# Text-side edits in a two-stream attention block: shift sums folded after block transposes, text V shifted at its eviction, and the text gate's matmuls in the output phase

## The chip, the cores and the metric

The kernel runs on one core of a Trainium2 chip. The metric is device time in microseconds (us), median of five runs. In the text PE is TensorE with its matmuls, PEld its weight loads, DVE is VectorE, ACT is ScalarE, POOL is GpSimd, and SP is the engine whose queue issues most DMAs.

## The reference

There are two streams of tokens: image (B = 2 batches of 256 tokens) and text (2 of 32), with D = 1152. Weights and inputs are bfloat16.

```python
mod_i = (_silu(c) @ wmod_img).reshape(B, 6, 1, D)
mod_t = (_silu(c) @ wmod_txt).reshape(B, 6, 1, D)
shi, sci, gai = mod_i[:, 0], mod_i[:, 1], mod_i[:, 2]
sht, sct, gat = mod_t[:, 0], mod_t[:, 1], mod_t[:, 2]
hi = _layernorm(x_img) * (1 + sci) + shi
ht = _layernorm(x_txt) * (1 + sct) + sht
qkvi, qkvt = hi @ wqkv_img, ht @ wqkv_txt
q, k, v = concat of text and image parts
p = _softmax(einsum('bqd,bkd->bqk', q, k) * D ** -0.5)
a = einsum('bqk,bkd->bqd', p, v)
out_i = x_img + gai * (ai @ wo_img)
out_t = x_txt + gat * (at @ wo_txt)
```

So each stream needs a shift, a scale and a gate, each the product of the two silu(c) rows with a 1152 x 1152 slice of its modulation weights.

## The kernel before, in words

All work is on one core. D is cut into KT = 9 blocks of 128. Weights of 1152 x 1152 (2.65 MB) come from DRAM into five slots (w0 to w4); SP issues their DMAs in the order of lines 100 to 122, and a DMA whose slot is still in use waits on SP, with all behind it. `pin` keeps instructions in program order on their engine, so PE's order is the order of the code. The accumulators in PSUM come from two pools, ps_mm (six buffers) and ps_tr (two).

The stages, in PE's order:

1. Image LayerNorm, transposes, image scale and V (lines 296 to 342, `v_open`, `v_last`). The image shift is left out of the V input, and added later: `shift_v_rows` (391) multiplies the shift by the V weights, keeps the rows in `svr` (bfloat16) and as columns in `cols["v"]`, which the evictions of the attention output add to all tokens (L623, L625).
2. Image Q and K, nine blocks each (`qk_img`, 372), with hooks between blocks for text work: statistics and norm (402 to 412), transposes (414), scale rows (`txt_rows_scale`), shift, modulation.
3. Text Q and K (`qk_txt`, 478), scores and softmax (lines 646 to 668), the image gate (`img_gate`) between them, text V (`v_txt`, 489), transposes of the probabilities (`p_transposes`, 594), the text gate (`txt_gate`, 526), attention (`attn_pair`, 628), and the output products (679 to 718).

**Modulation rows.** A 32-column stationary operand holds silu(c) in two columns; four column groups of the array work on four strips of the weights at a time (`mod_rows_of`, 334): 36 matmuls of 288 columns for one product. **The text shift** goes another way: DVE multiplies each of the nine weight blocks by a per-partition scalar and adds (L425, L427, 18 instructions of 128x1152 for the two batches), which leaves sums over 128 partitions to do. ACT and DVE split the float32 sums into a high and a low bfloat16 half (`vec_split`, 430), and PE adds over the partitions with a one-column `pick` operand, 16 matmuls of 288 columns (`vec_rows`, 438); DVE transposes the result into columns (L229, L462).

**Text V.** Because the eviction of the attention output adds the image's shift row to every token, the text's V must have it subtracted: `v_txt` does that with four matmuls of `sel` (entries -1) and `svr` into the same accumulators. `v_txt_out` copies four strips into `v_t`, and L674 repeats the rows at partition 64, so that `attn_pair` can use four row groups.

**The gates.** `mod_rows` (506): 36 matmuls, an ACT copy `g_sb`, two POOL DMAs into a DRAM scratch (L515), and then POOL DMAs that read it back broadcast over partitions: `gb` for the image (L524), `gbf` for the text (L533). `xf` is the text input for the residual (L529). `out_txt` uses gbf and xf at L707 and L708.

**The text softmax.** `scores_txt` sums even and odd blocks in two halves of the partitions; ACT copies one half (L654), DVE adds (L657), takes the maximum (L554), ACT the exponential (L561), DVE divides into `pb_txt`, tile `pbt` (L568, L570). `p_transposes(0)` and `(1)` both read it.

Of the kernel before, what the change touches and what calls it, by code (L numbers as in the profile page):

```python
# [9 lines left out]
ALU = mybir.AluOpType  # L10
# [4 lines left out]
def kernel(  # L15
# [21 lines left out]
    P = 128  # L37
# [55 lines left out]
    def load_rows(slot, src, c0):  # L93
        t = wtile(slot)
        sv = wview(src, c0)
        for r0 in range(0, KT, 3):
            nc.sync.dma_start(t[:, r0:r0 + 3, :], sv[:, r0:r0 + 3, :])
        return t
# [14 lines left out]
    w_sh_t = load_rows(0, wmod_txt, 0)  # L113
# [6 lines left out]
    w_ga_t = load_w(2, wmod_txt, 2 * D)  # L120
    w_o_i = load_rows(3, wo_img, 0)
    w_o_t = load_rows(1, wo_txt, 0)
# [22 lines left out]
    pick = const.tile([P, B, 32], bf)  # L145
    nc.gpsimd.memset(pick[:], 0.0)
    for b in range(B):
        nc.gpsimd.memset(pick[:, b, b:b + 1], 1.0)
# [13 lines left out]
    nc.gpsimd.tensor_copy(ident2[:, P - NT:P], ident[:, 0:NT])  # L162

# [63 lines left out]
    def mod_cols_of(gps, name):  # L227
        t = const.tile([P, KT, LW], f32, name=name, tag={"shtc": "scc", "sctc": "shc"}.get(name, name))
        pin(nc.vector.transpose(t[:].rearrange("p c l -> p (c l)"), gps[:].rearrange("p c l -> p (c l)")))  # L229
        return t  # L230
# [124 lines left out]
    pin(nc.scalar.dma_start(x_t[:], xt_flat[:, :]))  # L355
# [16 lines left out]
    def qk_img(wq, blk, hooks):  # L372
        for j in range(KT):
# [3 lines left out]
            for kt in range(KT):  # L377
# [5 lines left out]
    sel = const.tile([P, NGG, NTT], bf)  # L383
    nc.gpsimd.tensor_scalar(sel[:].rearrange("p g (b t) -> p g b t", b=B),
                            ident[:].rearrange("p (g r) -> p g r", g=NGG)[:, :, 0:B].unsqueeze(3)
                            .to_broadcast([P, NGG, B, NT]), -1.0, None, op0=ALU.mult)
    v_t = act.tile([P, D], bf)
# [3 lines left out]
    def shift_v_rows():  # L391
        p_sv = mod_rows_of(w_v_i, shT32)
        nc.scalar.copy(svr[:], p_sv[:])
        cols["v"] = mod_cols_of(p_sv, "svc")

# [6 lines left out]
    def txt_stats():  # L402
        junk = v_t[0:NTT, :]
        pin(nc.scalar.activation(junk, x_t[:], ACT.Copy, scale=1.0 / D, accum_out=sm_t[0:NTT, 0:1]))
        pin(nc.scalar.activation(junk, x_t[:], ACT.Square, scale=float(D) ** -0.5, accum_out=sm_t[0:NTT, 1:2]))

    def txt_norm():
        pin(nc.vector.scalar_tensor_tensor(sm_t[0:NTT, 2:3], sm_t[0:NTT, 0:1], sm_t[0:NTT, 0:1], sm_t[0:NTT, 1:2],
                                           op0=ALU.mult, op1=ALU.subtract))
        rstd = ln_rstd(sm_t[0:NTT, 2:3], NTT, sign=-1.0)  # L410
        for h, (c0, c1) in enumerate(((0, KH * P), (KH * P, D))):
            ln_norm(x_t[:, c0:c1], sm_t[0:NTT, 0:1], rstd, NTT, xn_t[NTT * h:NTT * (h + 1), 0:c1 - c0])
# [8 lines left out]
    def vec_part(eng, w, acc, r0, r1, bs):  # L421
        for kt in range(r0, r1):
            for b in bs:
                if kt == 0:
                    pin(eng.tensor_scalar(acc[:, b, :], w[:, kt, :], sTf[:, kt, b:b + 1], None, op0=ALU.mult))  # L425
                else:
                    pin(eng.scalar_tensor_tensor(acc[:, b, :], w[:, kt, :], sTf[:, kt, b:b + 1], acc[:, b, :],  # L427
                                                 op0=ALU.mult, op1=ALU.add))

    def vec_split(acc):  # L430
        hl = work.tile([P, 2, B, D], bf, tag="hl", bufs=1, name="hl")
        halves[acc.name] = hl
        for b in range(B):
            nc.scalar.copy(hl[:, 0, b, :], acc[:, b, :])
            pin(nc.vector.tensor_sub(hl[:, 1, b, :], acc[:, b, :], hl[:, 0, b, :]))
        return hl

    def vec_rows(hl, gps, strip):
        terms = [(b, t) for b in range(B) for t in range(2)]
        for b, t in terms:  # L440
            for g in range(NGG):
                mm(gps[LW * g:LW * g + LW], lhsT=pick[:, b, :], rhs=strip(hl[:, t, b, :], g),
                   start=((b, t) == terms[0]), stop=((b, t) == terms[-1]), tile_position=(0, LW * g))
        return gps

    halves = {}
    acc_sh = act.tile([P, B, D], f32, tag="Bt")

    def txt_shift_part(r0, r1):
        return lambda: vec_part(nc.vector, w_sh_t, acc_sh, r0, r1, range(B))  # L450

    def txt_shift_split():
        vec_split(acc_sh)

    def txt_rows_shift():
        gps = ps_tr.tile([P, KT, LW], f32, tag="tr")
        rows["sh"] = vec_rows(halves[acc_sh.name], gps,
                              lambda a, g: a.rearrange("p (c g l) -> p g c l", g=NGG, l=LW)[:, g])

    def txt_cols_shift():  # L460
        cols["sh"] = mod_cols_of(rows["sh"], "shtc")
        nc.vector.tensor_copy(mod_t[:, 0], cols["sh"][:, :, 0:B])  # L462
# [4 lines left out]
    def txt_modulate():  # L467
        cols["sc"] = mod_cols_of(rows["sc"], "sctc")
        nc.vector.tensor_scalar_add(mod_t[:, 1], cols["sc"][:, :, 0:B], 1.0)
        h = hT_t[:].rearrange("p kt (b t) -> p (kt b) t", b=B)  # L470
        nc.vector.tensor_mul(h, xT_t[:].rearrange("p kt (b t) -> p (kt b) t", b=B),
                             mod_t[:, 1].rearrange("p kt b -> p (kt b)").unsqueeze(2).to_broadcast([P, KT * B, NT]))
        nc.vector.tensor_add(h, h,
                             mod_t[:, 0].rearrange("p kt b -> p (kt b)").unsqueeze(2).to_broadcast([P, KT * B, NT]))
# [14 lines left out]
    def v_txt(r):  # L489
        ps = ps_mm.tile([P, KT, LW], f32, tag="mm")  # L490
        for kt in range(KT):
            for g in range(2):
                mm(ps[64 * g:64 * g + NTT], lhsT=hT_t[:, kt, :], rhs=group(w_v_t, kt, 2 * r + g),
                   start=(kt == 0), stop=False, tile_position=(0, 64 * g))
        for g in range(2):
            mm(ps[64 * g:64 * g + NTT], lhsT=sel[:, 2 * r + g, :], rhs=svr[:],
               start=False, stop=True, tile_position=(0, 64 * g))
        return ps

    def v_txt_out(r, ps):  # L500
        for g in range(2):
            dst = v_t[0:NTT, :].rearrange("p (c g l) -> p g c l", g=NGG, l=LW)[:, 2 * r + g]
            src = ps[64 * g:64 * g + NTT]
            pin(nc.vector.tensor_copy(dst, src))
# [16 lines left out]
    def img_gate():  # L521
        mod_rows(w_ga_i, 0)
        for b in range(B):
            nc.gpsimd.dma_start(gb[:, b, :], gsc[0, b, :].partition_broadcast(P))  # L524

    def txt_gate():
        mod_rows(w_ga_t, 1)
        for g in range(2):
            pin(nc.gpsimd.dma_start(xf[64 * g:64 * g + NTT, :, :],  # L529
                                    xt_flat.rearrange("t (r g j) -> g t r j", r=2, g=2)[g]))  # L530
            for b in range(B):
# [6 lines left out]
    qk_img(w_q_i, 0, {1: (txt_stats, txt_shift_part(0, 3),), 3: (txt_norm,), 4: (txt_shift_part(3, 6),),  # L538
                      7: (txt_shift_part(6, KT),)})
    qk_img(w_k_i, 1, {1: (txt_transposes, txt_shift_split,),  # L540
                      6: (txt_rows_scale, txt_rows_shift, txt_cols_shift, txt_modulate),
                      8: (lambda: qk_txt(0, w_q_t),)})
# [51 lines left out]
    def p_transposes(b):  # L594
        pT_ps = ps_tr.tile([P, 8 * P], bf, tag="tr")

        def one(kj, pb, qp, perm):
            o = kj * NTOK + qp
            tr(pT_ps[:, o:o + P], pb[:, kj * P:(kj + 1) * P], perm[:])

        for kj in range(3):
            if b:
                one(kj, pbs["t"], qpos[b][2], ident2)
            for qi in range(TPB):
                one(kj, pbs[(b, qi)], qpos[b][qi], ident)
            if not b:
                one(kj, pbs["t"], qpos[b][2], ident)
        pT_v = pT_ps[:, 0:3 * NTOK].rearrange("p (k n) -> p k n", k=3)
        pT = work.tile([P, 3, NTOK], bf, tag="pT")
        pin(nc.scalar.copy(pT[:], pT_v))  # L610
# [17 lines left out]
    def attn_pair(ids0, ids1):  # L628
# [3 lines left out]
        for n, key in enumerate([x for pair in zip(t0, t1) for x in pair]):  # L632
            first, (b, dt) = key in t1, key
            r0 = 64 * (n // 2 % 2) + NT * b
            mm((t1 if first else t0)[key][:], lhsT=v_t[r0:r0 + NT, dt * P:(dt + 1) * P],
# [15 lines left out]
    soft_exp(I[1])  # L651
    st = scores_txt()
    half = work.tile([NTT, NTOK], f32, tag="half", bufs=1)
    pin(nc.scalar.copy(half[:], st[NTT:P, :]))  # L654
    img_div(I[1])
    img_gate()
# [12 lines left out]
    vt = [v_txt(r) for r in range(2)]  # L669
    v_txt_out(0, vt[0])  # L670
    p_transposes(0)
    p_transposes(1)
    v_txt_out(1, vt[1])
    pin(nc.vector.tensor_copy(v_t[64:64 + NTT, :], v_t[0:NTT, :]))  # L674
    txt_gate()
    for d0 in range(0, KT, 3):
        attn_pair(*[[(b, dt) for dt in range(d0, d0 + 3)] for b in range(B)])

    def out_img(i, chunks, parts=None):
# [4 lines left out]
        for n in chunks:  # L684
            ps = ps_mm.tile([P, CH], f32, tag="mm")
# [29 lines left out]
    out_img(1, C3)  # L715
# [33 lines left out]
```

## Time and profile before

| what | us |
|---|---|
| median of five runs | 119.0 (118.69 to 119.22) |
| the profiled execution | 118.93 |
| its span | 117.1 |
| PE busy | 110.8 (95%), 1046 matmuls |
| PE weight loads | 64.0 (55%) |
| DVE busy | 74.6 (64%) |
| ACT busy | 44.4 (38%) |
| POOL busy | 11.1 (10%) |
| DMA moved | 40.86 MB, mean 349 GB/s |

The page cuts the span in 40 slices and gives the busy share of each engine in tenths; PEclk is the clock granted to TensorE. The chain that ended last is followed back from the last instruction, and its shares tell on which engine it ran. The timeline gives start, duration, engine, line and shapes of each group; the idle time of the engine before it stands in brackets with what ended it. Times in a timeline are us from the span's start. A list of DMAs gives the time from issue to landing.

### The profile page before, as it was taken

Reading aid. Unit: us, or ns where it says so; the run is one execution under the profiler, and the core shown is the slowest. Engines: PE = TensorE matmul, PEld = TensorE weight load, DVE = VectorE, ACT = ScalarE, POOL = GpSimd, SP = SyncE. Lnnn points to the kernel's source line nnn. Section 1 sums busy time; section 2 is a strip of 40 time slices with the busy share of each in tenths; the row PEclk is TensorE's granted clock in tenths of the full one; section 3 lists DMA queues with packets and bytes.
Section 4 is the critical chain, followed back from the end, with each engine's and each line's share of the span. In section 5 each row is a group of like instructions: output and inputs, shape, how many; then the busy total and the mean of one; then the engine's idle time right before and its main releaser. Section 6 shows DMA issues by size and latency. Waiting matters only on the chain.

```text
span 117.1 us, 2513 instructions
## 1 busy us (share of the span) xinstructions
PE 110.8 (95%) x1046; PEld 64.0 (55%) x1054; DVE 74.6 (64%) x158; ACT 44.4 (38%) x91; POOL 11.1 (10%) x34
## 2 busy tenths in 40 slices
PE   4998799999999999999999999999999999999990
PEld 1245544445584444444444648777885666666660
DVE  2478395053865997999999350018994756666671
ACT  4799520031654815325248224245556620000000
POOL 7320000000000000000000000001309017000000
PEclk9999999999999999999999999999999999999999
DMA  3999999999999999999999999999999999420223
GB/s 118 388 376 398 404 406 408 414 412 412 412 400 372 412 410 412 406 410 414 412 411 412 412 406 410 413 408 408 411 403 412 406 395 348 147 101 6 101 50 101
DMA packets 18613, 40.86 MB, mean 349 GB/s; under 512 B 1019, under 2 KB 1547, under 8 KB 18603
## 3 DMA queue, kind: packets, MB, share of 16 engines
q1 hardware_dynamic: 17728, 39.56, 86.8%
q0 software_dynamic: 480, 0.89, 2.1%
q10 hardware_dynamic: 395, 0.26, 0.7%
q8 instruction: 8, 0.13, 0.4%
q14 instruction: 2, 0.02, 0.0%
HBM read 39.38 MB, written 1.34 MB: 348 GB/s over the span
## 4 chain that ended last, share of the span: by engine, by line
PE 85%; DMA 9%; DVE 1%; SPq 1%; issue 1%; DVEq 0%
PE ps L61 53%; PE vps L61 15%; DMA t<-in_wmod_img_dram 9%; PE gps L61 6%; PE aps L61 5%; PE sps L61 4%; PE pT_ps L64 1%; PE sc_ps L61 1%; SPq L104 1%; PE tp L64 1%; DVE tmp L690 1%; DVE o L691 0%; SPq L108 0%; PE tpt L64 0%; DVE hS_i L268 0%
## 5 line engine op out<-in xcount | busy, mean ns | idle before, releaser
L61 PE MATMUL ps<-xT_i,t 128*128 128x512 bf16 x157 | 35.2, 379 | 0.4 <-issue 0.2
L61 PEld LDWEIGHTS <-t 128*128 128x128 bf16 x324 | 20.5, 98 | 19.1 <-issue 0.5
L427 DVE SCALAR_TENSOR_TENSOR acc_sh<-t,sTf,acc_sh 128x1152 f32<-128x1152 bf16 x16 | 21.4, 1412 | 0.0
L61 PE MATMUL ps<-t,aT 128*128 128x384 bf16 (+3 forms) x153 | 20.2, 308 | 0.0
L61 PE MATMUL vps<-t,hS_i 128*128 128x512 bf16 (+1 forms) x106 | 17.8, 325 | 0.2
L61 PEld LDWEIGHTS <-aT 128*128 128x128 bf16 (+1 forms) x153 | 13.0, 101 | 7.1 <-issue 0.5
L61 PEld LDWEIGHTS <-hS_i 128*128 128x128 bf16 x108 | 9.0, 98 | 8.7 <-DVE hS_i L268 0.4
L690 DVE TENSOR_TENSOR tmp<-ps,gb 128x384 bf16<-128x384 f32 (+2 forms) x13 | 6.8, 525 | 6.4 <-PE ps L61 6.3
L370 ACT CAST qkT<-ps 128x512 bf16<-128x512 f32 (+2 forms) x11 | 6.0, 552 | 10.4 <-PE ps L61 10.4
L515 POOL DMA_DIRECT2D mod_scratch<-g_sb x4 | 2.5, 634 | 75.0 <-ACT g_sb L513 74.9
L368 ACT ACTIVATE qkT<-ps 128x512 bf16<-128x512 f32 (+2 forms) x11 | 6.0, 557 | 8.6 <-PE ps L61 8.6
L61 PE MATMUL wps<-warm 128*128 128x512 bf16 x24 | 7.7, 478 | 1.7 <-DVE unit L132 1.5
L184 DVE CAST v_i<-vps 128x512 bf16<-128x512 f32 x5 | 3.5, 692 | 7.5 <-PE vps L61 7.5
L554 DVE TENSOR_REDUCE nmx<-sps 128x1 f32<-128x288 f32 x4 | 1.8, 457 | 9.9 <-PE sps L61 9.9
L61 PEld LDWEIGHTS <-sT 128*32 128x32 bf16 x180 | 4.7, 96 | 3.0 <-issue 2.3
L186 ACT CAST v_i<-vps 128x512 bf16<-128x512 f32 x4 | 2.3, 578 | 9.9 <-PE vps L61 9.9
L623 DVE TENSOR_SCALAR aT<-aps,svc 128x288 bf16<-128x288 f32 x9 | 4.3, 518 | 2.5 <-PE aps L61 2.5
L61 PE MATMUL sps<-qkT 128*128 128x288 bf16 (+1 forms) x54 | 5.5, 287 | 0.0
L61 PEld LDWEIGHTS <-warm 128*128 128x128 bf16 x25 | 2.6, 115 | 5.2 <-issue 2.4
L61 PE MATMUL gps<-t,sT 128*32 128x288 bf16 x144 | 5.2, 287 | 0.0
L61 PE MATMUL aps<-pT,v_i 128*128 128x288 bf16 x36 | 5.1, 287 | 0.0
L61 PE MATMUL ps<-hT_t,t 128*128 128x64 bf16 x162 | 5.0, 193 | 0.0
(114 smaller groups left out, 109.2 us busy)
## 6 DMA issues: line engine op xcount, KB each, us to landing
t<-in_wqkv_txt_dram SPq DMA_DIRECT2D x3, 2592.0 KB, 18.0
t<-in_wmod_img_dram SPq DMA_DIRECT2D x2, 2592.0 KB, 12.6
t<-in_wqkv_img_dram SPq DMA_DIRECT2D x2, 2592.0 KB, 20.2
t<-in_wmod_txt_dram SPq DMA_DIRECT2D x2, 2592.0 KB, 16.2
t<-in_wmod_txt_dram SPq DMA_DIRECT2D x3, 864.0 KB, 15.2
t<-in_wo_img_dram SPq DMA_DIRECT2D x3, 864.0 KB, 13.1
t<-in_wo_txt_dram SPq DMA_DIRECT2D x3, 864.0 KB, 12.7
t<-in_wqkv_img_dram SPq DMA_DIRECT2D x3, 576.0 KB, 8.7
```

The costliest lines, as they stand in the source:

```text
L61: return pin(nc.tensor.matmul(*a, **k))
L64: return pin(nc.tensor.transpose(*a, **k))
L104: nc.sync.dma_start(x_i[:, b * TPB:(b + 1) * TPB, :], x_img[b].rearrange("(p t) d -> p t d", t=TPB))
L184: nc.vector.tensor_copy(out_ap, in_ap)
L186: nc.scalar.copy(out_ap, in_ap)
L368: nc.scalar.mul(out_ap, in_ap, SCALE)
L370: nc.scalar.copy(out_ap, in_ap)
L427: pin(eng.scalar_tensor_tensor(acc[:, b, :], w[:, kt, :], sTf[:, kt, b:b + 1], acc[:, b, :], op0=ALU.mult, op1=ALU.add))
L515: nc.gpsimd.dma_start(gsc[si, b, :].rearrange("(g j) -> g j", g=NGG), g_sb[b:P:32, :])
L554: pin(nc.vector.reduce_max(nmx[0:qn, :], sps[0:qn, :], axis=AX.X, negate=True))
L623: nc.vector.tensor_scalar(dst, tiles[(b, dt)][:], bias, None, op0=ALU.add)
L690: nc.vector.tensor_mul(tmp[:, 0:n], ps[:, 0:n], gb[:, b, c0:c0 + n])
```

## The change

- **Shift sums.** The nine blocks of products stay on DVE (`shift_part`). Then DVE transposes the float32 sums in 32 x 32 blocks and reduces along the free axis (`shift_blocks`), which leaves 36 partial sums for each batch and partition. These 72 columns are split in two bfloat16 parts, and two matmuls of 72 columns with a constant `fold` add over the four groups of 32 partitions; a mask `band` and a reduce pick the right column (`shift_fold`). The 16 pick matmuls, the ACT and DVE splits and one transpose go.
- **Place of the text modulation.** The scale rows come ahead of K block 4 (before: 6), the scale product follows `shift_blocks` on DVE, and fold and shift come ahead of K block 8. Text K now follows image K directly; text Q comes after the first two image scores; the image gate comes ahead of the text scores.
- **Text V.** `svr` goes through a DRAM scratch (POOL DMAs, L401 and L405 of the changed kernel) to `svb`, one row broadcast to the text's partitions. `v_txt` has no sel matmuls, reads contiguous columns and splits them over two halves of the partitions; one DVE subtraction for each accumulator (and a 64 x 64 one) writes `v_t`. The attention takes the output blocks in another order, (0, 5, 1), (6, 2, 7), (3, 8, 4), for the new layout.
- **Probability transposes.** `p_transposes(0)` comes before `v_txt`, `p_transposes(1)` after it, the latter in two tiles with two ACT copies, its third key block first.
- **Text gate.** `txt_gate` is called between the first and second chunk of `out_img(1)`; `xf` is loaded with the image gate.
- **Loads.** The text shift weights come in four DMAs instead of three; x_t comes on SP's queue behind them (before: ACT's queue); wo_img comes ahead of the text gate's weights and in slot 4; wo_txt in two DMAs.
- **Text LayerNorm.** The two normalizing instructions go from DVE to ACT.

```diff
+    w_sh_t = load_rows(0, wmod_txt, 0, (0, 1, 3, 6))
+    nc.sync.dma_start(x_t[:], xt_flat[:, :])
...
-    w_ga_t = load_w(2, wmod_txt, 2 * D)
-    w_o_i = load_rows(3, wo_img, 0)
-    w_o_t = load_rows(1, wo_txt, 0)
+    w_o_i = load_rows(4, wo_img, 0)
+    w_ga_t = load_w(3, wmod_txt, 2 * D)
+    w_o_t = load_rows(1, wo_txt, 0, (0, 5))
...
+    fold = const.tile([P, NGG, LW], bf)
+    nc.gpsimd.tensor_add(fold[:, 0, :], ident[:, 0:LW], ident[:, LW:2 * LW])
...
+        for b in range(B):
+            nc.gpsimd.dma_start(svd[b].rearrange("(c g l) -> g c l", g=NGG, l=LW), svr[b:P:LW])
+        for g in range(2):
+            for b in range(B):
+                r0 = 64 * g + NT * b
+                nc.gpsimd.dma_start(svb[r0:r0 + NT, :], svd[b, g * HD:(g + 1) * HD].partition_broadcast(NT))
...
+    def shift_blocks():
         for b in range(B):
+            blk = work.tile([P, NB, LW], f32, tag="blk", bufs=1, name="blk")
+            pin(nc.vector.transpose(blk[:].rearrange("p c l -> p (c l)"), acc_sh[:, b, :]))
+            pin(nc.vector.reduce_sum(uf[:, b, :], blk[:], axis=AX.X))
+        pin(nc.vector.tensor_copy(ub[:, 0], uf[:]))
+        pin(nc.vector.tensor_sub(ub[:, 1], uf[:], ub[:, 0]))
+
+    def shift_fold():
+        ps = ps_tr.tile([P, B * KT, NGG], f32, tag="tr", name="shps")
+        for h in range(2):
+            mm(ps[:].rearrange("p k a -> p (k a)"), lhsT=fold[:].rearrange("p g l -> p (g l)"),
+               rhs=ub[:, h].rearrange("p b c -> p (b c)"), start=(h == 0), stop=(h == 1))
+        pin(nc.vector.tensor_mul(uf[:].rearrange("p b (k a) -> p (b k) a", a=NGG), ps[:],
+                                 band[:].unsqueeze(1).to_broadcast([P, B * KT, NGG])))
+        pin(nc.vector.reduce_sum(mod_t[:, 0].rearrange("p k b -> p b k"),
+                                 uf[:].rearrange("p b (k a) -> p b k a", a=NGG), axis=AX.X))
...
     def v_txt(r):
-        ps = ps_mm.tile([P, KT, LW], f32, tag="mm")
+        ps = ps_mm.tile([P, VC], f32, tag="mm")
         for kt in range(KT):
             for g in range(2):
-                mm(ps[64 * g:64 * g + NTT], lhsT=hT_t[:, kt, :], rhs=group(w_v_t, kt, 2 * r + g),
-                   start=(kt == 0), stop=False, tile_position=(0, 64 * g))
-        for g in range(2):
-            mm(ps[64 * g:64 * g + NTT], lhsT=sel[:, 2 * r + g, :], rhs=svr[:],
-               start=False, stop=True, tile_position=(0, 64 * g))
+                c0 = g * HD + r * VC
+                mm(ps[64 * g:64 * g + NTT, :], lhsT=hT_t[:, kt, :], rhs=w_v_t[:, kt, c0:c0 + VC],
+                   start=(kt == 0), stop=(kt == KT - 1), tile_position=(0, 64 * g))
         return ps
 
     def v_txt_out(r, ps):
...
+        pin(nc.vector.tensor_sub(v_t[:, r * VC:(r + 1) * VC], ps[:], svb[:, r * VC:(r + 1) * VC]))
...
-    qk_img(w_k_i, 1, {1: (txt_transposes, txt_shift_split,),
-                      6: (txt_rows_scale, txt_rows_shift, txt_cols_shift, txt_modulate),
-                      8: (lambda: qk_txt(0, w_q_t),)})
+    qk_img(w_k_i, 1, {1: (txt_transposes,), 4: (txt_rows_scale, shift_blocks, txt_scale),
+                      8: (shift_fold, txt_shift)})
     qk_txt(1, w_k_t)
...
+    qk_txt(0, w_q_t)
+    img_div(I[1])
+    img_gate()
     st = scores_txt()
...
-    img_div(I[1])
-    img_gate()
...
-    vt = [v_txt(r) for r in range(2)]
-    v_txt_out(0, vt[0])
     p_transposes(0)
+    for r in range(2):
+        v_txt_out(r, v_txt(r))
     p_transposes(1)
-    v_txt_out(1, vt[1])
-    pin(nc.vector.tensor_copy(v_t[64:64 + NTT, :], v_t[0:NTT, :]))
-    txt_gate()
...
     out_img(0, C3)
-    out_img(1, C3)
+    out_img(1, C3, between=txt_gate)
     out_img(2, C3)
     out_txt()
```

## The prediction

> **What bounds the kernel now.** First the page: the span in slices, then the chain that ended last.
>
> ```profile
> PE   4998799999999999999999999999999999999990
> ...
> DVE  2478395053865997999999350018994756666671
> ...
> PEclk9999999999999999999999999999999999999999
> DMA  3999999999999999999999999999999999420223
> ...
> PE 85%; DMA 9%; DVE 1%; SPq 1%; issue 1%; DVEq 0%
> ```
>
> TensorE (PE) is busy in every slice but the first and last, at full clock, and 85% of the chain is PE. In order of time the chain stays on PE from 14.67 us to 113.48 us, with gaps of 0.05 us. So between these marks the end moves by what the change takes out of PE's sequence, plus any wait it puts in. The DMA engines are as full until 101 us, so each weight must still land in time. The profiled run took 118.93 us (span 117.1, 1.8 around it); the median shown is 119.0. I add to 118.93.
>
> Second, PE's timeline around the edits (start, duration, instruction):
>
> ```profile
> 64.39 1.29 PE L61 MATMUL gps<-t,sT 128*32 128x288 bf16 x36
> 65.50 0.66 PE L61 MATMUL gps<-hl,pick 128*32 128x288 bf16 x16
> ...
> 69.99 2.52 PE L61 MATMUL ps<-hT_t,t 128*128 128x64 bf16 x81
> ...
> 80.78 2.38 PE L61 MATMUL sps<-qkT 128*128 128x288 bf16 x18
> 83.09 1.29 PE L61 MATMUL ps<-t,hT_t 128*64 128x288 bf16 x18
> 84.22 0.29 PE L61 MATMUL ps<-svr,sel 128*64 128x288 bf16 x2
> 84.34 1.27 PE L61 MATMUL ps<-t,hT_t 128*64 128x288 bf16 x18
> 85.44 0.29 PE L61 MATMUL ps<-svr,sel 128*64 128x288 bf16 x2
> 85.67 0.29 PE L64 MATMUL pT_ps<-ident,pb 128*128 128x128 bf16 x2
> ```
>
> A duration includes the pipeline's tail, so I count from start to start. Third, the VectorE (DVE) timeline of the text softmax:
>
> ```profile
> 80.81 0.45 DVE L657 TENSOR_TENSOR half<-sps,half 64x288 f32<-64x288 f32 x1
> 81.29 0.45 DVE L554 TENSOR_REDUCE nmx<-half 64x1 f32<-64x288 f32 x1
> ...
> 82.49 0.15 DVE L566 RECIPROCAL rs<-rs 64x1 f32<-64x1 f32 x1
> 82.68 0.39 DVE L568 TENSOR_SCALAR pbt<-e,rs 64x256 bf16<-64x256 f32 x1
> 83.00 0.49 DVE L570 TENSOR_SCALAR pbt<-e,rs 32x64 bf16<-32x64 f32 x2
> ```
>
> From the add of the two halves to the last piece of the text probabilities pbt is 2.68 us. Its PE cover in the kernel before is the image scores (80.78) and all of v_txt (83.09 to 85.67).
>
> **Shift sums.** The scale rows and the 16 pick matmuls run from 64.39 to 66.09 (the next weight load): 1.70 us. 36 such matmuls alone take 1.22 (28.37 to 29.59), so the 16 cost 0.48. The two fold matmuls have 72 columns; the nearest row has 64, 81 in 2.36 us (69.99 to 72.35), 0.03 each, so 0.06; if nothing overlapped, two of 193 ns, 0.39. I take the lower end, since they stand in a full PE queue, in the whole-array form of their neighbours. Net **-0.42** (at worst -0.09).
>
> DVE must deliver. It starts on the first row of the weights at about 36 (its row shows it free at 35.90, waiting 1.10 for three rows), does two products (1.46) and 16 sums at a 1.34 pitch (21.4), and ends near 59.1. Two block transposes are bounded by 0.48 (288 elements) and 1.9 (four times that): between the 128- and 288-element rows the slope is 1.09 ns an element, so 1.42. Two reduces of 1152 by the slope of the 1.36 us subtraction: 1.36. With two small casts the partial sums stand at 65.0, at worst 66; the scale part adds 1.5. PE reaches the fold at 54.58 + 3 blocks of 1.943 + 0.1 + 1.22 + 4 blocks = 69.50: 3 to 4 us to spare. After it DVE has 0.23 + 0.25 + 0.76 (multiply, reduce, add; rows L570, L690, L473) under one block of 1.94 us, so hT_t is there about 0.35 us before PE asks at 71.50. Were that cover gone, 1.4 us would show. The Trainium skill, "VectorE: DVE Perf Modes", section "Rules for kernel authors", speaks against a reduce on a hot path, as the slowest DVE operation. The row is 0.457 us for 288 elements, which agrees; by either the slack above holds the two.
>
> **V shift.** The four sel matmuls cost 84.34 - 84.22 = 0.12 and 85.67 - 85.44 = 0.23, of which 0.11 is the change to the next form of tile and stays: **-0.24**. The shift rows go through DRAM and back from 36 on; the rows for such pairs take 7 + 5 us, the use is at 84. The subtraction is a tensor_tensor like L707 (0.46) and replaces two copies of 0.45 and the copy L674 (0.45): off PE.
>
> **Order around the softmax.** Text Q (81 matmuls, 2.36) goes behind the first scores and the gate ahead of the text scores: the same PE work. I count six changes of tile form from there to the output phase's end in both orders, so they cancel. In "TensorEngine Tiling (Array Packing)", "Key Properties", the skill says that a change of tiling mode drains TensorE; the weight loads here sit idle 0.24 us at each. PE then runs: text K 71.50, scores 73.86, text Q 76.02, gate 78.50, text scores 79.59, image scores 80.32, and at 82.48 the transposes of batch 0, which now come before v_txt. They need pbt. The text scores' tail ends at 80.38 (79.59 + 0.79, as 78.96 to 79.75); ScalarE copies a half by 80.81, the add starts at 80.84, and by the rows above the first 256 columns end at 83.10 and the last 32-row pieces at 83.52. PE gets to the first pbt transpose at 82.59 and to the third about 0.33 us later. It waits 0.56 + 0.09: **+0.65**. Bounds: 0 if pbt is in time; 1.0 if the first transpose also waits for the last pieces. v_txt, now 2.23 us, and everything else are queued behind the transposes on PE.
>
> **Gate of the text.** 36 matmuls leave the place where they covered ScalarE's probability copies (86.38 to 88.04). There v_txt covers the first copy. The second is split: by the rows 0.40 (288) and 0.65 (between 0.40 and 0.88) it ends at 87.6, with PE needing it at 87.7: 0, at worst 0.2. In the output phase the gate's 1.22 us stands bare: **0** in sum. What it costs is a deadline. Gate at 98.37, tail 99.76, ScalarE copy to 100.2, GpSimd (POOL) issues at 100.5 and 101.1. These rows bound the round trip:
>
> ```profile
> mod_scratch<-g_sb POOLq DMA_DIRECT2D x1, 2.2 KB, 7.0
> ...
> gbf<-mod_scratch POOLq DMA_DIRECT2D x1, 36.0 KB, 3.6
> ```
>
> 7.0 under full DMA load, 3.6 at 98 us when the load falls; the load ends at 101, so I take 3.3 (3.0 to 3.6) for the write. Four reads issue behind it at 0.55 pitch and land at 108.5 to 109.4; DVE wants gbf at 108.1. DVE then has 1.64 (text) + 1.92 (two image chunks) ahead of the chunk it starts at 113.48, so the end moves only if gbf lands after 109.9: 0 in the forecast, one for one beyond. "DMA: Bandwidth & Descriptors", "Anatomy of one DMA", gives a fixed cost of about 2.0 us; by it gbf would land near 107 and nothing would wait. The rows here are longer.
>
> **Loads.** Landings, asked stretch by stretch:
>
> ```profile
> t<-in_wqkv_txt_dram SPq DMA_DIRECT2D x1, 2592.0 KB, 14.2
> ...
> t<-in_wmod_txt_dram SPq DMA_DIRECT2D x1, 2592.0 KB, 13.5
> ```
>
> Text K is issued at 52.55 and lands at 66.75; it is now needed at 71.50 (before: 74.30). The text gate's weights landed at 86.05 for 86.77; wo_img's last third, issued at about 79.4, landed 14.3 us later, near 93.7, for 94.75. The swap of the two lands wo_img some 6 us earlier and the gate's near 94 for 98.37. On SP's in-order queue wo_txt is issued 0.4 us later, for a use at 107. x_t, now behind the shift weights, lands near 41.5; ScalarE asks at 41.3, and DVE's variance, which needs it, comes at 46. x_t (144 KB) and the shift rows (0.15 MB) take 0.7 us of stream at 410 GB/s, under slacks of 4 us. All 0. The LayerNorm moved to ScalarE, and POOL's constants ahead of 5.49, lie beside PE.
>
> **Sum.** -0.42 - 0.24 + 0.65 = -0.01: 118.92 on that run, **119.0** as a median.
>
> **Rivals.** *Softmax in time (faster).* The wait at the transposes is under 0.3 us and the removed matmuls count: 118.93 - 0.66 + 0 to 0.3 = 118.3 to 118.6. For it: DVE's text chain has one image division fewer in front of it; against: every row of that chain is serial.
> *Gate round trip (slower).* gbf lands after 109.9 and DVE, in order, holds the last image chunks. With 4.2 us in place of 3.3 for the write and 3.8 for the read gbf lands near 110.5: +0.6, 119.5; with the 5.3 that the same write took at 81.6 and a read of 4.5, near 112.2: +2.3, 121.2. For it: two DRAM trips in series with 8 us; against: the load ends at 101.
> *Late text chain (slower).* The transposes wait 1.0, or hT_t or the second copy misses: +0.35 to +0.8, 119.3 to 119.8.
> *Nothing saved:* the pick and sel matmuls ran beside other work. PE's starts show them in line, so I give it no chance of its own.
>
> **Chances.** Forecast 0.35 (its own range 118.65 to 119.35), softmax in time 0.31, round trip 0.19, late chain 0.15. A measurement can tell about 0.3%, 0.36 us, from no change; so faster 0.31, same 0.35, slower 0.34. Range 118.3 to 119.9: it reaches over most of both sides and leaves the slow round trip out.
>
> **What would show it.** Between the scale rows and the next block: 1.22 us. v_txt start to the transposes of batch 1: 2.3. PE idle of about 0.6 at the first pbt transpose, released by DVE. DVE waiting for a DMA at the first text output product, without a gap on PE. No DMA wait on PE. I am wrong if PE idles at text K, if the attention's first tiles wait for ScalarE, or if the last chunk is released by DVE and not by PE.

## The result, and the profile after

| | kernel before | changed kernel |
|---|---|---|
| median, us | 119.05 (117.90 to 119.45, 85 runs) | 119.46 (118.65 to 119.93, 43 runs) |
| the profiled execution, us | 118.93 | 119.34 |
| its span, us | 117.1 | 116.9 |
| time minus span, mean over the runs | 1.81 (1.75 to 1.88) | 2.32 (1.91 to 2.49) |

The ratio is 1.0035, 95% interval 1.0026 to 1.0044: slower by 0.41 us. Times are of ordinary runs; a few at a lower clock or of some 400 us, k4's profiled one among them, are left out. The third and fourth rows hold the surprise: the span did not get longer, the time outside it did. "Time minus span" (below also "outside") is a run's time less the stretch from its first to its last traced instruction; the profile page shows nothing of it. For the kernel before it is taken over its runs beside the experiments below.

The page of the changed kernel, in slices, and the shares of its chain:

```profile
PE   4999899999999999999999999999899999999990
...
DVE  2478494053869999999999512153858666356671
...
PEclk9999999999999999999999999999999999999999
DMA  3999999999999999999999999999999999522223
...
PE 83%; DMA 8%; DVE 3%; SPq 1%; issue 1%; ACT 1%; DVEq 0%; ACTq 0%
```

PE is as full as before at the same clock. The chain has 3% DVE (before: 1%) and 1% ACT (before: none): between the first V matmul and PE's last one it now leaves PE once, for the text softmax. PE's timeline around the edits:

```profile
60.38 1.29 PE L61 MATMUL gps<-t,sT 128*32 128x288 bf16 x36
61.60 1.25 PE L61 MATMUL ps<-xT_i,t 128*128 128x512 bf16 x4
...
69.38 0.23 PE L61 MATMUL shps<-ub,fold 128*128 128x72 bf16 x2
69.44 2.11 PE L61 MATMUL ps<-xT_i,t 128*128 128x512 bf16 x9
71.39 2.53 PE L61 MATMUL ps<-hT_t,t 128*128 128x64 bf16 x81
...
82.45 0.28 PE L64 MATMUL pT_ps<-ident,pb 128*128 128x128 bf16 x2
83.05 0.23 PE L64 MATMUL pT_ps<-ident,pbt 128*128 128x128 bf16 x1 [0.32 <-DVE pbt L583]
...
83.62 2.40 PE L61 MATMUL ps<-t,hT_t 128*64 128x288 bf16 x36
85.95 0.23 PE L64 MATMUL pT_ps<-ident,pbt 128*128 128x128 bf16 x1
```

From start to start: the scale rows take 1.22 with no pick matmuls behind them, the fold 0.06, and text K follows at once. The transposes of batch 0 begin at 82.45, the first that needs pbt stands until 83.05, and v_txt starts at 83.62, 0.56 later than the nine transposes alone would let it (they take 0.61 where nothing waits: 1.17 - 0.61). v_txt takes 2.33 from there to the next transposes (85.95), where the kernel before took 2.58 (83.09 to 85.67). DVE's part of that wait:

```profile
80.77 0.45 DVE L669 TENSOR_TENSOR half<-sps,half 64x288 f32<-64x288 f32 x1 [2.78 <-ACT half L668]
81.25 0.45 DVE L569 TENSOR_REDUCE nmx<-half 64x1 f32<-64x288 f32 x1
...
82.65 0.34 DVE L583 TENSOR_SCALAR pbt<-e,rs 64x256 bf16<-64x256 f32 x1
```

The gate's trip through DRAM, from the list of DMAs between 95 and 112 us (size, us from issue to landing), and the text output on DVE:

```profile
gbf<-mod_scratch POOLq DMA_DIRECT2D x4, 36.0 KB, 2.4
...
mod_scratch<-g_sb POOLq DMA_DIRECT2D x2, 2.2 KB, 2.0
```

```profile
108.16 0.46 DVE L718 TENSOR_TENSOR tmp<-ps,gbf 128x288 bf16<-128x288 f32 x1 [0.28 <-PE ps L61]
```

The write took 2.0; the last of the four reads was issued at 104.4 and none took over 2.9, so gbf was there by about 107, and DVE at 108.16 waited for PE alone. The list of PE's waits over the whole span has 1.5 for `unit` at the start and 0.32 for pbt, and none for a DMA.

From the first V matmul to PE's last one the kernel before takes 98.79 (14.67 to 113.46), the changed one 98.69 (14.55 to 113.24): -0.10, where the forecast had -0.01. The 0.41 is outside.

Taken to the start of the last matmul, this stretch is 99.06 and 98.96, and it hardly scatters: it is 99.06 in the traces of three small additions to the kernel before (g2b, k2, n1 below) and 98.96 in those of five versions of the changed one (e2, g2a, k3, m1, m2). The time ahead of the first V matmul does scatter, from 13.75 to 14.67 over these and the other traces. So a mean span over some ten runs can be off by tenths, and the stretch is the better measure of what an edit does to PE.

### The profile page after: what moved, and what is told of

It reads as the page before. It is cut to its first block, busy times and chain, and to the rows that moved or that the text cites. A ratio compares the mean times of both kernels' runs of the same rounds, so it can differ in the third digit from the quotient of the medians.

```text
span 116.9 us, 2501 instructions
## 1 busy us (share of the span) xinstructions
PE 111.1 (95%) x1029; PEld 63.8 (55%) x1036; DVE 75.3 (64%) x158; ACT 44.8 (38%) x93; POOL 15.3 (13%) x47
## 3 DMA queue, kind: packets, MB, share of 16 engines
HBM read 39.52 MB, written 1.34 MB: 349 GB/s over the span
## 4 chain that ended last, share of the span: by engine, by line
PE 83%; DMA 8%; DVE 3%; SPq 1%; issue 1%; ACT 1%; DVEq 0%; ACTq 0%
PE ps L61 53%; PE vps L61 15%; DMA t<-in_wmod_img_dram 8%; PE gps L61 5%; PE aps L61 5%; PE sps L61 2%; PE pT_ps L64 1%; PE sc_ps L61 1%; SPq L104 1%; PE tp L64 1%; DVE tmp L701 1%; DVE o L702 0%; ACT e L576 0%; DVE half L669 0%; DVE nmx L569 0%
## 5 line engine op out<-in xcount | busy, mean ns | idle before, releaser
L61 PE MATMUL wps<-warm 128*128 128x512 bf16 x24 | 8.5, 518 | 1.7 <-DVE unit L133 1.5
L401 POOL DMA_DIRECT2D sv_scratch<-svr x2 | 1.8, 884 | 28.2 <-ACT svr L398 28.2
```

What stands on the lines that cost most here:

```text
L61: return pin(nc.tensor.matmul(*a, **k))
L401: nc.gpsimd.dma_start(svd[b].rearrange("(c g l) -> g c l", g=NGG, l=LW), svr[b:P:LW])
```

## Experiments inside the span

**e1_vtxt_first**: v_txt's first product ahead of the transposes, so that PE has work while the softmax ends.

```diff
+    vt0 = v_txt(0)
     p_transposes(0)
-    for r in range(2):
-        v_txt_out(r, v_txt(r))
+    v_txt_out(0, vt0)
+    v_txt_out(1, v_txt(1))
```

> The changed kernel with the first half of v_txt ahead of the transposes of batch 0, so that PE has 1.1 us more work before it needs the text probabilities. Theory A (the trace's: the wait of about 0.6 us for pbt at these transposes eats the saved matmuls): the wait goes, the span is 0.5 to 0.6 us shorter than the changed kernel's, near 116.5 against spans of 117.1 to 117.2, and the time about 118.9. Rival B (the wait only hides another limit, such as the copies of the probabilities or the loads): the span stays within 0.15 us. Theory C (the loss lies outside the span, in the six more DMAs that POOL issues) says nothing against A here: time minus span stays at the changed kernel's 2.3 us.

Measured: 118.57 against 118.59 of the kernel before on the same chip, ratio 0.9991 (0.9973 to 1.0009); mean span -0.61, time minus span 2.29. PE's timeline:

```profile
82.06 1.29 PE L61 MATMUL ps<-t,hT_t 128*64 128x288 bf16 x18
83.29 0.28 PE L64 MATMUL pT_ps<-ident,pb 128*128 128x128 bf16 x2
83.41 0.22 PE L64 MATMUL pT_ps<-ident,pbt 128*128 128x128 bf16 x1
...
83.89 1.29 PE L61 MATMUL ps<-t,hT_t 128*64 128x288 bf16 x18
```

The third transpose runs 0.12 behind the first and the wait is gone. So the wait was the softmax, and the product in front hides it. PE's stretch is 98.61: 0.35 less than in the changed kernel, and not the whole 0.56. Text V in two pieces has two more changes of tile form; at the prediction's 0.11 each, an estimate, they account for the rest. Against the kernel before the stretch is 0.45 shorter, as the rival "softmax in time" had it; the time hardly falls, since 0.48 comes back outside.

**e4_before_fold_only**: the kernel before with `shift_part`, `shift_blocks`, `shift_fold` and their places alone; text Q follows image K, text V, gates and loads stay.

> The kernel before with the folded shift sums alone (block transposes, reduces, two fold matmuls; scale rows ahead of K block 4; text Q after image K). The pick matmuls and the two splits are gone, softmax, v_txt and the gate stay as before. Theory A: PE loses 0.42 us and gains no wait, so span and time fall by 0.4 us, to about 118.65. Rival (the fold or its DVE chain comes too late for text Q at 71.4 us): 0 to +0.5 us, with PE waiting for DVE there. Theory C: time minus span stays at 1.85, since POOL issues ten DMAs as before.

Measured: ratio 0.9996 (0.9971 to 1.0022), mean span -0.17, time minus span 1.90. Its chain of work (start, duration):

```profile
60.34 1.22 PE gps L61 x36
61.56 7.88 PE ps L61 x36
69.44 0.07 PE shps L61 x2
69.50 6.67 PE ps L61 x171
76.17 2.93 PE sps L61 x36
```

From its first V matmul (14.44) to the image scores (76.17) are 61.73, in the kernel before 62.15 (14.67 to 76.82): -0.42, the forecast's figure. PE's whole stretch is 98.63, -0.43. The mean span does not show the 0.4 that was expected; its -0.17 lies in the scatter of the start.

**e3_before_plus_sv_trip** puts the six DMAs of the shift row's trip on the kernel before, with nobody reading their result; **e2_no_sv_trip** takes them from the changed kernel (svb is set to 0, so text V stays unshifted).

```diff
-        for b in range(B):
-            nc.gpsimd.dma_start(svd[b].rearrange("(c g l) -> g c l", g=NGG, l=LW), svr[b:P:LW])
-        for g in range(2):
-            for b in range(B):
-                r0 = 64 * g + NT * b
-                nc.gpsimd.dma_start(svb[r0:r0 + NT, :], svd[b, g * HD:(g + 1) * HD].partition_broadcast(NT))
+        nc.gpsimd.memset(svb[:], 0.0)
```

> The kernel before with the same six POOL DMAs added at the same place, their result unused. Theory C: the span stays at 117.1 and time minus span rises from 1.85 to about 2.3, so the time rises by 0.4 (ratio 1.0035). Rival D: no change within 0.15 us, since nothing on the chain waits for these DMAs.

> The changed kernel without the six POOL DMAs that carry the shift row through DRAM: svb is set to zero, so V of the text is not shifted and the text part of the result leaves that out. Everything else stays. Theory C (the part of the time outside the span grows with the number of DMAs that POOL issues, 10 before and 16 after): time minus span falls from 2.3 to about 1.85 us, the span stays within 0.15, the time falls by 0.4 to about 119.05. Rival D (the loss is inside the span and the profiled execution was a short one): time minus span stays at 2.3 and the time within 0.15 of the changed kernel.

Measured: e3 1.0053 (1.0031 to 1.0075), span +0.58, time minus span 1.81. e2 1.0033 (1.0016 to 1.005), span -0.22, time minus span 2.42. So the DMAs are not what lies outside. But e3 shows a cost that the forecast had no term for. The chain of e3:

```profile
77.26 2.83 SPq L97
80.09 0.05 issue
80.14 14.97 DMA t<-in_wo_img_dram
95.11 0.04 issue
95.15 18.70 PE ps L61 x138
```

In the kernel before the output phase starts at 93.94 and needs the last third of wo_img at about 94.75, a microsecond after it has landed (93.7 in the prediction). In e3 it lands at 95.11 and PE waits; its stretch is 99.46, +0.40. **g2b_before_sp_plus1** (the kernel before, wo_txt in four DMAs instead of three) had +0.45 in the mean span (ratio 1.0037, 1.0015 to 1.0058) at an unchanged 1.82 outside. Its trace has no such wait and the same stretch of 99.06; the difference lies behind PE's last matmul, from whose start to the span's end it is 3.82 us and in the kernel before 3.40. SP's program ends with eight waits for DMAs in a fixed order. In the kernel before seven are passed earlier and the eighth 2.52 us after that start; in g2b the first is passed at 2.52, and the seven others follow in 0.42. The changed kernel loads wo_img ahead of the gate's weights and pays none of this.

## Experiments outside the span

Several theories were tried in turn for the 0.5 us outside. C: the number of POOL's DMAs (e2 and e3 refute it). S: the length of SP's program. P: the length of PE's. A: ACT's and POOL's. D: DVE's. E: the last transfer on ACT's queue.

**g2a_after_sp_minus1**, **g2b_before_sp_plus1** and **g3_after_pe_longer**: the changed kernel with wo_txt in one DMA, the kernel before with it in four, and the changed kernel with 18 more matmuls of 8 columns.

```diff
-    w_o_t = load_rows(1, wo_txt, 0, (0, 5))
+    w_o_t = load_rows(1, wo_txt, 0, (0,))
```

> The changed kernel with wo_txt in one DMA instead of two, so that SP's program is one instruction shorter, as long as in the kernel before. The six POOL DMAs are cleared of the loss (with them added to the kernel before, time minus span stayed 1.82; with them taken out of the changed kernel it stayed 2.41). The trace goes on behind the span: the engines reset semaphores, then a chain of nine semaphore steps closes. In the two changed kernels looked at one of its steps takes 0.46 us where the kernel before has 0.10. Theory S (the step waits for more of SP's program, which has grown past a boundary): time minus span falls from 2.4 to about 1.95, the span stays near 116.6 to 116.8. Rival P (the length of PE's program, 2074 rows against 2110, decides): it stays at 2.4.

> The kernel before with wo_txt in four DMAs instead of three, so that SP's program is one instruction longer. Theory S: time minus span rises from 1.81 to about 2.3 and the time by 0.45, with the span unchanged. Rival P, or any theory in which the work inside the span decides: no change within 0.15 us.

> The changed kernel with 18 more 8-column matmuls in PE's idle time at 11 to 12 us, which makes PE's program as long as in the kernel before (2110 rows). Rival P: time minus span falls from 2.4 to about 1.9. Theory S: it stays at 2.4. The span stays within 0.2 us by both.

Ratios 1.0043 (1.0017 to 1.0069), 1.0037 and 1.006 (1.0034 to 1.0087). Outside 2.35, 1.82 and 2.19, the first and the third in two groups of runs (near 2.0 and near 2.45). S falls, and P too, since the upper group is still there, though in three of g3's eight runs only (in the changed kernel in 37 of 44).

**h1_best**: e1 with wo_txt in one DMA, the mask `band` by one DVE reduction, and the four reads of svb in two DMAs (POOL 59 traced instructions). **k1_act_pool_trimmed**: the same with wo_txt in two DMAs and ACT two instructions shorter; **k3_after_act_minus2** has that last edit alone:

```diff
-        pin(nc.scalar.activation(sm_t[0:NTT, 1:2], sm_t[0:NTT, 0:1], ACT.Copy, scale=rstd[0:NTT, :]))
+        pin(nc.vector.tensor_mul(sm_t[0:NTT, 1:2], sm_t[0:NTT, 0:1], rstd[0:NTT, :]))
...
-            eng = nc.sync if g == 0 else nc.scalar
-            eng.dma_start(ot_flat.rearrange("t (r g j) -> g t r j", r=2, g=2)[g], of[64 * g:64 * g + NTT, :, :])
+            nc.sync.dma_start(ot_flat.rearrange("t (r g j) -> g t r j", r=2, g=2)[g], of[64 * g:64 * g + NTT, :, :])
```

**k2_before_act_plus2** and **k4_before_pool_plus16** put two ACT copies, and sixteen POOL memsets, of one column each at the start of the kernel before.

> The candidate for a faster version: the changed kernel with the first half of v_txt ahead of the transposes of batch 0, wo_txt in one DMA, the band mask made by one DVE reduce instead of five POOL instructions, and svb read back by two POOL DMAs instead of four (POOL's program falls from 65 to 58 traced instructions). Theory S: span near 116.2, time minus span 1.85, time 118.05, a ratio of 0.9955 to the kernel before. Rival P: time minus span stays at 2.3, time 118.5, ratio 0.999.

> The changed kernel with text V's first product ahead of the transposes, ScalarE two instructions shorter (traced count 107 instead of 109) and GpSimd six shorter (59 instead of 65), the weights of the text output still in two transfers. Theory A (the time outside the span grows when ScalarE's program passes a length between 108 and 109 traced instructions, and a little more when GpSimd's passes one between 59 and 65): time minus span 1.8 to 1.9 us instead of 2.3, span 0.5 to 0.6 under the kernel before as with text V moved alone, so the time 0.4 to 0.6 us under the kernel before (ratio 0.995 to 0.997). Rival U (the time outside the span has to do with something else of the change, such as the folded sums or the gate at the end of the stream): time minus span stays at 2.2 to 2.4 and the ratio is 0.998 to 1.001.

> The kernel before with two ScalarE copies of one column each that nobody reads, at the start, where ScalarE waits for c: traced ScalarE count 110 instead of 108. Theory A: span unchanged within 0.15 us, time minus span 2.1 to 2.4 instead of 1.81, so the time 0.3 to 0.5 us longer. Rival U: time minus span stays at 1.8 to 1.9, ratio 0.999 to 1.002.

> The changed kernel with ScalarE two instructions shorter and nothing else (107 instead of 109; GpSimd stays at 65): the small scaling of the text mean goes to VectorE, one output transfer goes to SyncE's queue. Theory A: time minus span falls from 2.38 to 1.9 to 2.0, what is left over 1.81 being GpSimd's part; span unchanged within 0.15 us; the time 0.4 us under the changed kernel's, about 119.0 where the kernel before gives 118.5 to 119. Rival U: time minus span stays at 2.3 to 2.4 us.

> The kernel before with sixteen GpSimd memsets of one column each that nobody reads, at the start: traced GpSimd count 66 instead of 50. Theory A's smaller part: time minus span 1.95 instead of 1.81, with the third block of semaphores reset some 0.5 us later after the span's end (1.34 instead of 0.81); span unchanged within 0.15 us; the time 0.1 to 0.2 us longer. Rival U: time minus span stays at 1.81 and the third block is reset at 0.81 us.

| run | ratio | span less before's | outside |
|---|---|---|---|
| h1_best | 1.0012 (0.9986 to 1.0038) | -0.19 | 2.16 |
| k1_act_pool_trimmed | 1.0032 (1.0007 to 1.0057) | -0.31 | 2.48 |
| k2_before_act_plus2 | 0.9986 (0.9964 to 1.0009) | -0.13 | 1.82 |
| k3_after_act_minus2 | 0.9989 (0.9965 to 1.0014) | -0.37 | 2.01 |
| k4_before_pool_plus16 | 1.002 (0.9992 to 1.0048) | -0.14 | 2.11 |

ACT's length is not it: k2 lengthens it and nothing moves, k1 shortens it and has 2.48. POOL's counts: k4 has +0.30 outside from memsets that no one waits for. And k3's small edit took the outside of the changed kernel from 2.32 to 2.01.

k1's profile also shows the rival "gate round trip" at work:

```profile
99.89 4.57 DMA mod_scratch<-g_sb
...
106.39 3.74 DMA gbf<-mod_scratch
...
110.26 0.47 DVE tmp L716
```

gbf lands at 110.13, DVE's text product starts 2.1 later than in the changed kernel, and the chain reaches the end by DVE's queue and not by PE. From PE's last matmul to the span's end are 3.83 us (changed kernel: 3.41), so the late gate costs 0.4. In the list of DMAs the write's median is 4.4 here, 4.3 in h1 and 2.0 in the changed kernel; in the ten other versions with a trace of this write at the end of the stream it is 1.9 to 3.4. k1's stream was not over: from 101 to 103 us it still moved 354 and 203 GB/s, in the changed kernel 112 and 1. Both h1 and k1 read svb in two DMAs instead of four; that this is the cause was not tested.

**m1_after_dve_plus2**, **m2_after_out_on_sp** take k3 apart: two DVE memsets that no one reads (DVE 188 as in k3); the output transfer alone. **m3_vtxt_first_act_minus2** is e1 with k3's edit, **m4_vtxt_first_dve188** the same with the two memsets.

```diff
+    idle = small.tile([P, 2], f32, bufs=1, name="idle")
+    for i in range(2):
+        nc.vector.memset(idle[:, i:i + 1], 0.0)
```

> The changed kernel with two VectorE memsets of one column each that nobody reads, at the start: traced VectorE count 188 instead of 186, as in the changed kernel with ScalarE shortened, where time minus span came out at 2.00. Theory D (the length of VectorE's program decides: 186 is long outside the span, 188 is not): time minus span 2.0 instead of 2.3 to 2.4, span unchanged within 0.15 us, so the time falls by 0.3 to 0.4 although two instructions were added. Theory E (the end of ScalarE's or SyncE's program decides, through the output transfer): time minus span stays at 2.3 to 2.4.

> The changed kernel with one edit of the two: the second half of the text output leaves by SyncE's queue instead of ScalarE's (traced ScalarE 108, SyncE 69; VectorE unchanged at 186). Theory D: time minus span stays at 2.3 to 2.4. Theory E: it falls to 2.0. Span unchanged within 0.15 us by both.

> Text V's first product ahead of the transposes, and ScalarE two instructions shorter, both on the changed kernel (traced VectorE 186, GpSimd 65). Span by both theories 0.5 to 0.6 under the kernel before, as with text V moved alone. Theory D: time minus span 2.3 to 2.4 (VectorE 186), ratio about 1.000. Theory E: time minus span 2.0, ratio about 0.997.

> The same with two VectorE memsets that nobody reads (traced VectorE 188, GpSimd 65, ScalarE 107). Theories D and E both: time minus span 2.0, span 0.5 to 0.6 under the kernel before, the time 0.3 to 0.4 us under the kernel before, ratio 0.997: the version that should beat both. If time minus span is again 2.3 to 2.5, neither length decides alone.

Ratios 1.0025 (1.0001 to 1.0049), 1.0004 (0.9979 to 1.003), 0.9986 (0.9957 to 1.0016), 0.9984 (0.996 to 1.0008). Outside 2.08, 2.11, 2.32, 2.05; mean spans against the kernel before -0.03, -0.19, -0.54, -0.34. m1 bears D out as to the time outside: two useless instructions took 0.24 off, and the group of runs near 2.4 is gone, as in k3 and m4. E is half right and D not the whole: m2, with DVE at 186, lies between (1.92 to 2.30). m3, with DVE at 186, has both groups again.

**m5_vtxt_first_pool_short** is m4 with POOL at 58: `band` by a DVE reduction, three copies of `fold` in one.

> The changed kernel with text V's first product ahead of the transposes, ScalarE two instructions shorter, VectorE at a traced count of 188, and GpSimd back at 58 (its band mask by one VectorE reduction, the three copies of the fold matrix in one), the shift's DMAs as in the changed kernel. Theory D with GpSimd's part: both parts of the time outside the span are gone, time minus span 1.8 to 1.95; span 0.4 to 0.6 under the kernel before; the time 0.3 to 0.55 us under it, ratio 0.9955 to 0.9975. If time minus span stays at 2.0 to 2.1, VectorE at 188 itself has a price of 0.2 outside the span and GpSimd's part does not add to it; ratio 0.997 to 0.999. If it is 2.3 or more, no single length decides.

Measured: 118.11 against 118.6, ratio 0.9967 (0.994 to 0.9995); mean span -0.59 (PE's stretch -0.45), outside 2.00. The second of the three expectations: DVE at 188 has its own price, and POOL's part does not add to it. This is the lowest ratio of the eighteen versions tried, and its interval just leaves out 1.

**n1_before_dve_plus6** gives the kernel before the DVE count of the changed one, 186, by six memsets.

> The kernel before with six VectorE memsets of one column each that nobody reads, at the start: traced VectorE count 186 instead of 180, as in the changed kernel. If VectorE's length alone carries the larger part of the changed kernel's time outside the span, time minus span is 2.2 to 2.4 instead of 1.81 and the time 0.4 to 0.55 us longer, ratio 1.003 to 1.005. If it needs something else of the change beside it, time minus span is 1.8 to 1.95, as in the kernel before with the folded sums alone, which has 186 too; ratio 0.999 to 1.002. Span unchanged within 0.15 us by both.

Measured: ratio 1.0005 (0.9991 to 1.0019), outside 1.90, as e4, which has 186 too. DVE's length alone puts on 0.09, not 0.5.

What the trace holds beyond the span's end supports a cause there. Each execution ends with five blocks of semaphores being reset, then a chain of nine steps that closes the run. Start of two blocks, the chain's last step, and the instruction fetches after the end (us after the span's end), with the mean time outside and that of the traced execution:

```
traced counts             DVE ACT POOL  mean  traced  block 105  block 156  last step  fetches
before                    180 108  50   1.81  1.80    0.81       0.78       1.91       none
n1_before_dve_plus6       186 108  50   1.90  1.88    0.81       0.78       1.99       none
e2_no_sv_trip             184 109  59   2.42  2.44    0.81       0.78       2.29       none
changed kernel            186 109  65   2.32  2.42    1.34       0.77       2.06       1.80 to 2.37, 2.18 to 2.65
e1_vtxt_first             184 109  65   2.29  2.32    1.33       0.77       2.42       2.03 to 2.35
k1_act_pool_trimmed       185 106  59   2.48  2.58    0.81       0.78       1.95       2.25 to 2.82
m3_vtxt_first_act_minus2  186 106  65   2.32  1.95    1.33       0.77       2.05       1.80 to 2.12
m1_after_dve_plus2        188 109  65   2.08  2.11    1.33       1.26       2.05       1.77 to 2.30, 1.80 to 2.35
m5_vtxt_first_pool_short  188 106  58   2.00  2.02    0.81       1.28       1.98       1.74 to 2.26
```

Block 105 starts half a microsecond late in every one of the nine profiles with POOL at 65, and in none with 50 to 59; block 156 in all four with DVE at 188, and in none with 180 to 186. So the length of an engine's program does reach past the end, in steps. The group of runs near 2.3 to 2.5 is seen only in versions of the changed kernel with DVE at 184 to 186, and not in all of these (m2); in four of them (the changed kernel, g2a, g3, m3) it comes and goes by about 0.45 us from run to run.

The same table tells what sets the time. In 17 of the 19 traces the time outside is, within 0.03 us, the later of two figures: the chain's last step less 0.10, and the end of the last fetch less 0.24. (Both offsets are read off these traces, 0.10 off the kernel before, which has no fetch, 0.24 off k1.) In the changed kernel the chain alone would give 1.96, and the fetch that ends at 2.65 gives 2.41; measured 2.42. g2a and g3, traced in the upper group, have such a fetch from 2.19; m3, traced in the lower, has not. In m1 the last fetch starts at 1.80 and not at 2.18, so the two memsets gain. This is a match of marks in traces and not an experiment on the fetches. e2 and h1 do not fit: their traces show no fetch after the end, and their time is 0.24 and 0.36 longer than the chain's figure.

**What stays open.** No single length sets the 0.5: POOL's carries up to 0.30 (k4), DVE's 0.09 (n1), and k1 has 2.48 with POOL and ACT both short. Which engine fetches so late in the upper group, why only in some runs, and what holds e2 and h1 was not settled.

## Why the prediction was wrong, point by point

- **Shift sums, -0.42**: right (e4: -0.42 from V to the image scores). DVE's blocks were in time (partial sums at 64.6, forecast 65.0): PE went from the fold to K block 8 and to text K without a wait. Two readings were loose: PE's chain has one gap of 0.16 (at 66.17) beside those of 0.05, and the 0.457 us of the reduce does not show it slower than other DVE work, since the add of the same length takes 0.45.
- **V shift, -0.24, and the softmax wait, +0.65**: the wait was 0.56, and text V took 2.33 where it took 2.58, -0.25. With the fold's -0.42 these give about -0.1, which is what PE's stretch changed by. The rows do not show 0.24 of idle weight loads "at each" change of tile form; at 86.77 it is 0.10.
- **Gate, 0 in sum**: right, though the write was quicker than the forecast's 3.3. It took 2.0 in the changed kernel's trace, 1.9 to 3.4 in ten other versions, and gbf was there by about 107, not 108.5 to 109.4. The rows chosen (7.0 and 3.6) were of transfers beside a full stream. The Trainium skill, "DMA: Bandwidth & Descriptors", "Anatomy of one DMA", gives a fixed cost of about 2.0 us; the changed kernel's trace agrees with it (2.0), while most of the other versions lie above it, up to 4.4 in k1.
- **Loads, all 0**: right for the changed kernel. What the forecast did not say is that the kernel before had a microsecond to spare with wo_img and no more (e3).
- **"Span 117.1, 1.8 around it"**: this is the step that failed. The sum was made on 118.93 with the 1.8 as a constant, and the steps worked only inside the span. The 1.8 is now 2.3, and that is the whole of the +0.41 (0.51 outside, about -0.1 inside). In the traced executions it went from 1.80 to 2.42, where the closing chain ends 0.15 later and an instruction fetch ends later still. The forecast had no rival for it either; the slower side was given to the gate and the text chain, and in the changed kernel neither happened.
- **The rival "softmax in time"** priced the removal of the wait at 118.3 to 118.6. m5, which has that and part of the outside back, is at 118.11 where the kernel before has 118.6.

The section "The ~15µs preamble/postamble breakdown" of the Trainium skill's "Runtime: NRT & Kernel Launch" says that after a kernel each engine resets 51 semaphores; the blocks 105 and 156 are that (105 to 155, 156 to 206). Its section "Instruction fetch mechanics" calls the cost of crossing a block of instructions mostly hidden. The runs here differ: fetches after the end appear in the changed kernel and not in the kernel before, and the time outside goes from a mean of 1.81 to as much as 2.48.

## What to carry to other kernels

Look at time minus span before trusting a sum made inside the span: it was 1.75 to 1.88 us over all runs of the kernel before and up to 0.67 more, as a mean, in versions of the changed one, and edits off every critical path (16 memsets on POOL, two on DVE) moved it by +0.30 and -0.24. When a change is worth under half a microsecond, count the instructions it adds to each engine, and price a version with a few more or fewer before judging the idea. Judge an edit inside the span by the stretch of the engine that bounds it, which repeats to a few hundredths here, and not by the span, whose start scatters by 0.9. Where a chain of small serial steps must end before PE goes on, put an independent product between, as e1 does (0.35 of a wait of 0.56 gained).

## What the runs showed of the hardware that was not expected

- The end of a run depends on program lengths: block 105 at 1.34 us after the end with POOL at 65 traced instructions, 0.81 with 59; block 156 at 1.26 with DVE at 188, 0.77 with 186.
- Longer can be shorter: two more DVE instructions took 0.24 us off (2.32 to 2.08), in the traces with a last fetch from 1.80 instead of 2.18.
- The time outside the span matches the later of the closing chain's last step and the last instruction fetch in 17 of 19 traces, within 0.03 us.
- The same 2.2 KB write to DRAM at 100 us took 2.0 us in the changed kernel and 4.4 in k1, where the load stream was still running.
- Six small transfers of POOL, read by no one, cost the kernel before 0.58 us of mean span; in the trace 0.40 of PE's stretch, through a weight load that had a microsecond of slack.
- SP's closing waits come in a fixed order: one more DMA put the last landing first in it and the span's end 0.42 us later (g2b).
